# Decay attention followed by a token and channel mixer: w1 is loaded and converted one place later, and the token sums begin in pair 5

## The chip, the core and the metric

The kernel runs on one core of one Trainium2 chip. The metric is the device time of one execution in microseconds (us). The runs shown of the kernel before are 551.95, 554.14 and 551.8 us; their median is 551.95. Profiles come from one execution taken by the hardware profiler; its times are counted from the start of its span.

## The reference

Inputs are q, k and v of shape (4 batches, 8 heads, 768 positions, 64), one decay per head, and four weights. All are float32. The first half is attention with a decay and no softmax, in blocks of 64 positions:

```python
intra = einsum('bhic,bhjc->bhij', qb, kb) * Dmask          # lam ** (i - j) below the diagonal
out   = einsum('bhij,bhjd->bhid', intra, vb) + einsum('bhid,bhde->bhie', qb * lam_pow, kv_state)
kv_state = lam_block * kv_state + einsum('bhsd,bhse->bhde', kb * rev_pow, vb)
```

The heads are laid side by side into x of shape (4, 768, 512), and the second half is a mixer:

```python
h  = relu(x.T @ w_tok1) @ w_tok2         # over positions: w_tok1 (768, 256), w_tok2 (256, 768)
u  = x + h.T
h2 = relu(u @ w_ch1) @ w_ch2             # over channels: w_ch1 (512, 1536), w_ch2 (1536, 512)
out = u + h2
```

w_tok1 and w_tok2 are called w1 and w2 below. They come as 64-bit floats, and the kernel makes float32 of them itself.

## The kernel before

**Pairs and places.** Two heads of one batch are a *pair*; there are 16, four for each batch. The loop from line 671 runs i from -2 to 15; one turn of it is called *place i* here. Place i does the scores of pair i+1 (`scores`), the outputs of pair i (`from_states`, `outputs`), the running state of pair i+1 (`state`), the turning of k and q of pair i+2 (`turn_k`, `turn_q`, `turn_q_rows`), and the turning back of pair i's outputs (`turn_back`). The scores `sc`, the outputs `xT`, the states `kv`, the turned tiles `kt`, `qt` and `xp`, and the sums `ph` and `pu` are PSUM tiles. Pair i's output goes to `uT` of its batch (4 x 768 words in each partition).

**Precision.** Products of the mixer are made of three products each: a high part times a high part, low times high, high times low. So each operand exists as a high and a low tile. `turn_back` writes the turned outputs as `xhi` (ScalarE, line 391) and `xlo` (VectorE, line 392). They are in tiles for two pairs each, tags `xhi` and `xlo` with two buffers; the tiles of pairs 4 and 5 are the third of each tag and reuse those of pairs 0 and 1.

**Token sums.** A first-layer sum (`token_hidden`, line 479) is 18 matmuls of 128x256 for 128 hidden rows and half of the channels of one batch; it needs the turned outputs of two pairs and the whole of w1 in `w1h`, `w1l`. Its result is split by ScalarE (line 483, `hh`) and VectorE (line 484, `hl`). The second layer (`pu`, line 516) is added to `uT`. The table `take` says how many of these groups run in each place, `early` how many of them ahead of the first turning back.

**w1 and w2.** w1 comes in three parts of 512 KB (`load_w1`, line 430) to `uT` of batch 3, which nothing else uses yet. `convert_w1` makes float32 of a part: one step on ScalarE (line 410), four on VectorE (lines 411 to 420) in the space of `uT` of batch 1, and then the split into `w1h` (ScalarE, line 402) and `w1l` (GpSimd, line 403). w2 comes whole, 1.5 MB (`load_w2`, line 447), in place 3 to `uT` of batch 2, and goes through the same steps in three parts from place 5 on. The steps wait in the list `waiting`, and `later(n)` takes the next n of them between the other work.

**Order.** The order on each engine is that of the code; there is no scheduler for it. SP issues nearly all loads, one after the other: for each place v of pair i+3, then k and q of pair i+4. From pair 5 on q is loaded as four DMAs of 32 partitions and is turned by VectorE (line 227); before, TensorE turns it. A matmul that starts a PSUM tile waits until the bank's last reader is done:

```python
def bank(tag, nm, n):                    # line 82
    if tag == "sh" and spare:
        tag = spare.pop()
    return ps.tile([P, n], F32, tag=tag, bufs={"xT": 1, "sh": 3}[tag], name=nm)
```

`spare` gets the bank of the pair's first outputs once in each place, and the first turning of keys takes it.

**Operand tiles.** In place 10 `build` (line 633) begins to fill tiles for the channel mixer, among them `B11h0`, `B11l0`, `B21h0` and `B21l0` in the pool `up` (128 x 768 each). Nothing is in them before that.

Of the kernel before, what the change touches and what calls it, by code (L numbers as in the profile page):

```python
# [10 lines left out]
F32R = mybir.dt.float32r  # L11
# [11 lines left out]
def kernel(  # L23
# [25 lines left out]
    DM = H * D  # L49
    FT = w_tok1.shape[1]  # L50
    FC = w_ch1.shape[1]
    P = 128
    NC = S // P
# [318 lines left out]
    def turn_back(i, g):  # L372

        b, p = pairs[i]
        half = p // 2
        if p % 2 == 0 and g == 0:
            x_of[b, half] = [
                tokp.tile([P, NC, DM // 2], F32R, tag=t, bufs=2, name=f"{t}{b}{half}") for t in ("xhi", "xlo")
            ]
        xhi, xlo = x_of[b, half]  # L380
        xp = bank("sh", f"xp{i}{g}", 3 * P)
        for c in range(3):
            nc.tensor.transpose(  # L383
                out=xp[:, c * P : (c + 1) * P],
                in_=chunks_of(uT[b][:, p], g)[:, c],
                identity=ident,
            )
        hi = xhi[:, g::2, (p % 2) * P : (p % 2 + 1) * P]
        lo = xlo[:, g::2, (p % 2) * P : (p % 2 + 1) * P]
        src = xp.rearrange("p (c e) -> p c e", e=P)  # L390
        nc.scalar.copy(out=hi, in_=src)  # L391
        nc.vector.tensor_sub(out=lo, in0=src, in1=hi.bitcast(F32))  # L392
# [35 lines left out]
    def load_w1(i):  # L428
        cs = slice(2 * i, 2 * i + 2)
        nc.sync.dma_start(  # L430
            out=words(3).rearrange("p (c f) -> p c f", c=NC)[:, cs],
            in_=w_tok1.bitcast(U32).rearrange("(c s) f -> s c f", s=P)[:, cs],
        )
# [28 lines left out]
    def token_hidden(b, half, kk):  # L462

        if half == 0 and kk == 0:
            if b % 2:
                both = hidp.tile([P, 2, NK, DM], F32R, tag="h1", name=f"h{b}")
                hid[b] = both[:, 0], both[:, 1]
            else:
                hid[b] = [hidp.tile([P, NK, DM], F32R, tag=f"{t}0", name=f"{t}{b}") for t in ("hh", "hl")]
        hh, hl = hid[b]  # L470
        xh, xl = x_of[b, half]
        cs = slice(half * DM // 2, (half + 1) * DM // 2)

        ph = bank("sh", f"ph{b}{half}{kk}", DM // 2)
        fs = slice(kk * P, (kk + 1) * P)
        i = 0
        for c in range(NC):
            for w, x in ((w1h, xh), (w1l, xh), (w1h, xl)):
                nc.tensor.matmul(  # L479
                    out=ph, lhsT=w[:, c, fs], rhs=x[:, c], start=(i == 0), stop=(i == 3 * NC - 1)  # L480
                )
                i += 1
        nc.scalar.activation(hh[:, kk, cs], ph, AF.Relu)
        nc.vector.scalar_tensor_tensor(
            out=hl[:, kk, cs], in0=ph, scalar=0.0, in1=hh[:, kk, cs].bitcast(F32), op0=ALU.max, op1=ALU.subtract
        )
# [170 lines left out]
    groups = deque(hidden[0] + hidden[1][:NK] + outs[0] + hidden[1][NK:] + outs[1])  # L657
    for b in range(2, B):
        groups.extend(hidden[b] + outs[b])
    take = {4: 2, 5: 2, 6: 2, 7: 5, 8: 4, 9: 4, 10: 5, 11: 2, 12: 2, 13: 4, 14: 3, 15: 2}  # L660
    early = {4: 2, 5: 1, 6: 1}
    behind = []
    SCAN_FIRST = (5,)
    LATE = 7
# [9 lines left out]
    for i in range(-2, NI):  # L674
# [19 lines left out]
        if i + 2 < NI:  # L694
# [4 lines left out]
                turns += [(turn_q_rows, 0), (turn_q_rows, 1)]  # L699
            if i == -2:  # L700
                turns.sort(key=lambda x: x[1])
            if i >= NP and turns:
                behind.append(turns.pop())
            for f, g in turns:
                f(i + 2, g)
# [7 lines left out]
        for n in range(3):  # L713
# [11 lines left out]
            if n == 0 and i + 2 < NI:  # L725
                scale_k(i + 2)
                if i == LATE:
                    late_turns.popleft()(i + 2)
        if i == -1:
            load_w1(0)  # L730
        if 0 <= i + 3 < NI and i >= -1:
            load_v(i + 3)
        if i + 4 < NI:
            load_kq(i + 4)
        if i in (-1, 0):
            load_w1(i + 2)
        if i == 3:
            load_w2()
        if 0 <= i < 3:
            convert_w1(i)  # L740
        if i == 5:
            weights[0] = group_tiles(0, False)
            w3 = words(3)
# [648 lines left out]
```

## Time and profile before

| | |
|---|---|
| median of the runs | 551.95 us |
| the profiled execution's own time | 550.69 us |
| its span | 548.9 us |
| TensorE busy | 536.1 us (98%) |
| VectorE busy | 433.5 us (79%) |
| ScalarE, GpSimd busy | 255.3 us, 272.1 us |
| TensorE's clock | 1.00 of full speed in every stretch shown (the 2.4 GHz level) |

The chain of work that ended last is TensorE for 88% and VectorE for 5%. The first 165 us are the pairs with the token sums between them; the rest is the channel mixer. Rows of a timeline give start, length, engine, line, operation and tiles, and in brackets how long the engine had been idle before and what ended that. An engine "SPq" is SP's queue of DMA issues: the length is that of the issue, and the landing is told apart.

### The profile page before, as it was taken

How to read it: one execution, taken by the hardware profiler on the slowest of the kernel's cores; microseconds unless marked ns; L12 is line 12 of the kernel's file. 1: busy time of each engine (PE TensorE's matmuls, PEld its weight loads, DVE VectorE, ACT ScalarE, POOL GpSimd, SP SyncE). 2: the span in 40 equal slices, each digit the busy share in tenths (PEclk: the TensorE clock that was granted, in tenths of full speed). 3: DMA queues.
4: the chain of work that ended last, by engine and by line, in shares of the span. 5: the costliest groups of instructions: out<-in, count | busy, mean ns of one | idle time of the engine just before them, and what ended most of it. 6: DMA issues, size and time to landing. Idle time of an engine off the chain costs nothing.

```text
span 548.9 us, 11606 instructions
## 1 busy us (share of the span) xinstructions
PE 536.1 (98%) x4588; PEld 521.1 (95%) x4588; DVE 433.5 (79%) x658; ACT 255.3 (47%) x514; POOL 272.1 (50%) x242
## 2 busy tenths in 40 slices
PE   5999999999999999999999999999999999999997
PEld 4879998999989999999999999999999999999996
DVE  5697699588787988788778888788777778778894
ACT  3673553455453444443444344453455555455431
POOL 5574462745213564534444354354476656568450
PEclk9999999999999999999999999999999999999999
DMA  9999994998102614442716200014855132220276
GB/s 183 254 209 171 234 208 71 206 174 150 38 24 92 248 43 149 142 149 52 269 44 234 93 0 1 1 29 66 209 115 160 57 116 59 102 92 0 33 154 122
DMA packets 163142, 65.25 MB, mean 119 GB/s; under 512 B 151056, under 2 KB 153360, under 8 KB 163088
## 3 DMA queue, kind: packets, MB, share of 16 engines
q1 hardware_dynamic: 157856, 63.33, 47.5%
q10 hardware_dynamic: 5232, 1.18, 1.0%
q8 instruction: 36, 0.59, 0.5%
q14 instruction: 18, 0.15, 0.1%
HBM read 47.71 MB, written 16.78 MB: 117 GB/s over the span
## 4 chain that ended last, share of the span: by engine, by line
PE 88%; DVE 5%; DMA 2%; ACT 2%; POOL 1%; SPq 1%; issue 1%; ACTq 0%; DVEq 0%; POOLq 0%
PE po L1071 22%; PE pa L845 13%; PE pc L845 9%; PE pb L845 7%; PE pa L1045 7%; PE pc L1045 5%; PE ph L479 5%; PE sc L315 3%; PE xT L355 3%; PE pd L845 3%; PE pu L516 2%; PE pu L499 2%; DMA qn<-in_q_dram 1%; PE xT L338 1%; PE kv L267 1%; PE xp L383 1%
## 5 line engine op out<-in xcount | busy, mean ns | idle before, releaser
L1084 DVE TENSOR_TENSOR uT<-po,uT 128x768 f32<-128x768 f32 x57 | 54.2, 952 | 17.0 <-PE po L1071 16.7
L860 ACT ACTIVATE c<-c 128x384 f32<-128x384 f32 x42 | 22.1, 526 | 59.2 <-DVE c L905 33.4
L1051 DVE TENSOR_TENSOR uT<-pa,uT 128x768 f32<-128x768 f32 x36 | 34.3, 954 | 9.9 <-PE pa L1045 9.0
L862 POOL TENSOR_TENSOR h22l<-c,h22h 128x384 fp32r<-128x384 f32 x14 | 14.4, 1030 | 41.6 <-ACT h22h L861 41.6
L1051 DVE TENSOR_TENSOR uT<-pc,uT 128x768 f32<-128x768 f32 x27 | 25.8, 954 | 11.6 <-PE pc L1045 11.6
L286 POOL COPY st<-sv 128x320 f32<-128x320 f32 x16 | 13.6, 851 | 40.2 <-DVE sv L275 40.2
L298 DVE TENSOR_TENSOR a<-sc,mask 128x768 f32<-128x768 f32 x32 | 29.1, 947 | 4.3 <-PE sc L315 4.3
L403 POOL TENSOR_TENSOR c1l<-cs,c1h 128x512 fp32r<-128x512 f32 x15 | 19.3, 1296 | 23.1 <-ACT c1h L402 23.1
L1071 PE MATMUL po<-h12h,c 128*128 128x384 f32 x112 | 28.7, 337 | 0.0
L1071 PE MATMUL po<-h11h,c 128*128 128x384 f32 x112 | 28.6, 336 | 0.0
L1071 PE MATMUL po<-h21h,c 128*128 128x384 f32 x112 | 28.6, 336 | 0.0
L1071 PE MATMUL po<-h22h,c 128*128 128x384 f32 x112 | 28.6, 336 | 0.0
L479 PE MATMUL ph<-xhi,w1h 128*128 128x256 f32 x96 | 28.2, 293 | 0.1
L355 PE MATMUL xT<-a,vn 128*64 128x128 f32 x384 | 27.3, 277 | 0.0
L479 PE MATMUL ph<-xlo,w1h 128*128 128x256 f32 x96 | 27.1, 283 | 0.0
L479 PE MATMUL ph<-xhi,w1l 128*128 128x256 f32 x96 | 27.1, 282 | 0.0
L315 PE MATMUL sc<-qT,kT 64*64 64x128 f32 x768 | 25.2, 277 | 1.0 <-ACT xhi L391 0.8
L315 PEld LDWEIGHTS sc<-qT,kT 64*64 64x64 f32 x768 | 21.4, 136 | 4.2 <-issue 1.7
L254 POOL TENSOR_TENSOR qs<-qT,lamp 128x640 f32<-128x640 f32 x16 | 25.2, 1573 | 0.3 <-PE pu L516 0.2
L392 DVE TENSOR_TENSOR xlo<-xp,xhi 128x384 fp32r<-128x384 f32 x32 | 17.5, 551 | 7.4 <-ACT xhi L391 7.3
L355 PEld LDWEIGHTS xT<-a,vn 128*64 128x64 f32 x384 | 20.4, 137 | 3.0 <-issue 3.0
L403 POOL TENSOR_TENSOR c<-cs,c 128x512 fp32r<-128x512 f32 x10 | 12.9, 1295 | 19.7 <-ACT c L402 19.7
(399 smaller groups left out, 1942.9 us busy)
## 6 DMA issues: line engine op xcount, KB each, us to landing
raw<-in_moe_w_ch_dram SPq DMA_DIRECT2D x20, 512.0 KB, 3.7
vn<-in_v_dram SPq DMA_DIRECT2D x16, 384.0 KB, 5.1
kn<-in_k_dram SPq DMA_DIRECT2D x30, 192.0 KB, 5.6
out_dram<-y SPq DMA_DIRECT2D x104, 48.0 KB, 1.9
qn<-in_q_dram SPq DMA_DIRECT2D x44, 96.0 KB, 4.0
dc1h<-c1h SPq DMA_DIRECT2D x4, 768.0 KB, 5.3
dc1l<-c1l SPq DMA_DIRECT2D x4, 768.0 KB, 6.6
c1hr<-dc1h SPq DMA_DIRECT2D x4, 768.0 KB, 4.2
```

The lines of the kernel that those rows point to most:

```text
L254: nc.gpsimd.tensor_mul(out=qss[i], in0=qTs[i][:, P:].rearrange("p (c i) -> p c i", i=P), in1=lamp[:, p, None, :].broadcast_to([P, NC - 1, P]),
L298: nc.vector.tensor_mul(out=a, in0=pair.rearrange("p h (c i) -> p h c i", i=P), in1=mask[:, 2 * p : 2 * p + 2, None, :].broadcast_to([P, 2, ...
L315: nc.tensor.matmul(out=sc[h][half(j), c * P : (c + 1) * P], lhsT=kTs[i][half(h), js], rhs=qTs[i][half(h), cs], start=True, stop=True,)
L355: nc.tensor.matmul(out=xT[half((h + o) % 2), y * P : (y + 1) * P], lhsT=vns[i][:, h, c, :], rhs=weights_of[i, c // 3, h][:, c % 3, :], sta ...
L403: nc.gpsimd.tensor_sub(out=lo, in0=src, in1=hi.bitcast(F32))
L479: nc.tensor.matmul(out=ph, lhsT=w[:, c, fs], rhs=x[:, c], start=(i == 0), stop=(i == 3 * NC - 1))
L845: nc.tensor.matmul(out=to, lhsT=w[:, t], rhs=x[:, t], start=(start and i == 0), stop=(i == 5), skip_group_check=not start,)
L860: nc.scalar.activation(src, src, AF.Relu)
L1045: nc.tensor.matmul(out=pair[x][:, t], lhsT=w[:, t], rhs=h, start=(start and i == 0), stop=(i == 2), skip_group_check=not start,)
L1051: nc.vector.tensor_add(out=ub, in0=pair[x], in1=ub)
L1071: nc.tensor.matmul(out=to, lhsT=w[:, jj, t * P : (t + 1) * P], rhs=h, start=(i == 0), stop=(i == 3 * JG - 1))
L1084: nc.vector.tensor_add(out=ub, in0=po, in1=ub)
```

## The change

- w1: `load_w1` runs at the end of places -1, 0 and 1, each time behind the loads of v, k and q. Before, it ran in place -1 ahead of them and again behind them, and in place 0. `convert_w1` is called in places 1 to 3 and not 0 to 2.
- Sums: `take` has none in place 4 and three instead of two in places 5 and 6. The sums themselves and their order are the same; place 7 takes five as before. In place 4 both halves of the keys are turned ahead of the rest (`if i in take`).
- Tiles: the turned outputs of pairs 4 and 5 are not in `xhi`, `xlo` but in the four operand tiles named above, the even chunks of positions in one tile and the odd ones in another. `turn_back` and `token_hidden` index the tiles by chunk parity.

```diff
--- before.py
+++ after.py
@@ -374,9 +374,14 @@
         b, p = pairs[i]
         half = p // 2
         if p % 2 == 0 and g == 0:
-            x_of[b, half] = [
-                tokp.tile([P, NC, DM // 2], F32R, tag=t, bufs=2, name=f"{t}{b}{half}") for t in ("xhi", "xlo")
-            ]
+            if (b, half) == (1, 0):
+                x_of[b, half] = [
+                    [up.tile([P, NH, DM // 2], F32R, tag=f"{o}{x}0", name=f"x{o}{x}") for x in "hl"]
+                    for o in ("B11", "B21")
+                ]
+            else:
+                whole = [tokp.tile([P, NC, DM // 2], F32R, tag=t, bufs=2, name=f"{t}{b}{half}") for t in ("xhi", "xlo")]
+                x_of[b, half] = [[x[:, o::2] for o in range(2)] for x in whole]
         xhi, xlo = x_of[b, half]
         xp = bank("sh", f"xp{i}{g}", 3 * P)
         for c in range(3):
@@ -385,8 +390,8 @@
                 in_=chunks_of(uT[b][:, p], g)[:, c],
                 identity=ident,
             )
-        hi = xhi[:, g::2, (p % 2) * P : (p % 2 + 1) * P]
-        lo = xlo[:, g::2, (p % 2) * P : (p % 2 + 1) * P]
+        hi = xhi[g][:, :, (p % 2) * P : (p % 2 + 1) * P]
+        lo = xlo[g][:, :, (p % 2) * P : (p % 2 + 1) * P]
         src = xp.rearrange("p (c e) -> p c e", e=P)
         nc.scalar.copy(out=hi, in_=src)
         nc.vector.tensor_sub(out=lo, in0=src, in1=hi.bitcast(F32))
@@ -477,7 +482,7 @@
         for c in range(NC):
             for w, x in ((w1h, xh), (w1l, xh), (w1h, xl)):
                 nc.tensor.matmul(
-                    out=ph, lhsT=w[:, c, fs], rhs=x[:, c], start=(i == 0), stop=(i == 3 * NC - 1)
+                    out=ph, lhsT=w[:, c, fs], rhs=x[c % 2][:, c // 2], start=(i == 0), stop=(i == 3 * NC - 1)
                 )
                 i += 1
         nc.scalar.activation(hh[:, kk, cs], ph, AF.Relu)
@@ -657,8 +662,8 @@
     groups = deque(hidden[0] + hidden[1][:NK] + outs[0] + hidden[1][NK:] + outs[1])
     for b in range(2, B):
         groups.extend(hidden[b] + outs[b])
-    take = {4: 2, 5: 2, 6: 2, 7: 5, 8: 4, 9: 4, 10: 5, 11: 2, 12: 2, 13: 4, 14: 3, 15: 2}
-    early = {4: 2, 5: 1, 6: 1}
+    take = {5: 3, 6: 3, 7: 5, 8: 4, 9: 4, 10: 5, 11: 2, 12: 2, 13: 4, 14: 3, 15: 2}
+    early = {5: 1, 6: 1}
     behind = []
     SCAN_FIRST = (5,)
     LATE = 7
@@ -699,7 +704,7 @@
                 turns += [(turn_q_rows, 0), (turn_q_rows, 1)]
             if i == -2:
                 turns.sort(key=lambda x: x[1])
-            if i >= NP and turns:
+            if i in take and turns:
                 behind.append(turns.pop())
             for f, g in turns:
                 f(i + 2, g)
@@ -726,18 +731,16 @@
                 scale_k(i + 2)
                 if i == LATE:
                     late_turns.popleft()(i + 2)
-        if i == -1:
-            load_w1(0)
         if 0 <= i + 3 < NI and i >= -1:
             load_v(i + 3)
         if i + 4 < NI:
             load_kq(i + 4)
-        if i in (-1, 0):
-            load_w1(i + 2)
+        if -1 <= i < 2:
+            load_w1(i + 1)
         if i == 3:
             load_w2()
-        if 0 <= i < 3:
-            convert_w1(i)
+        if 1 <= i < 4:
+            convert_w1(i - 1)
         if i == 5:
             weights[0] = group_tiles(0, False)
             w3 = words(3)
```


On SP the three loads of w1 move. The names are those of the pair whose v, k or q is loaded (`vn3` is v of pair 3); `uT3` with `in_moe_w_tok1` is a part of w1. Before, from the end of place -1 to that of place 1:


```order
L430 DMA uT3_63<-in_moe_w_tok1_dram 128x2x512
L157 DMA vn2_243<-in_v_dram 128x12x64
L137 DMA kn3_245<-in_k_dram 128x6x64 x2
L140 DMA qn3_246<-in_q_dram 128x6x64 x2
L430 DMA uT3_63<-in_moe_w_tok1_dram 128x2x512
L157 DMA vn3_365<-in_v_dram 128x12x64
L137 DMA kn4_367<-in_k_dram 128x6x64 x2
L140 DMA qn4_368<-in_q_dram 128x6x64 x2
L430 DMA uT3_63<-in_moe_w_tok1_dram 128x2x512
L157 DMA vn4_494<-in_v_dram 128x12x64
L137 DMA kn5_496<-in_k_dram 128x6x64 x2
L115 DMA qn5_497<-in_q_dram 32x24x32 x4
```


The same stretch with the change, to the third part of w1:


```order
L157 DMA vn2_242<-in_v_dram 128x12x64
L137 DMA kn3_244<-in_k_dram 128x6x64 x2
L140 DMA qn3_245<-in_q_dram 128x6x64 x2
L435 DMA uT3_63<-in_moe_w_tok1_dram 128x2x512
L157 DMA vn3_364<-in_v_dram 128x12x64
L137 DMA kn4_366<-in_k_dram 128x6x64 x2
L140 DMA qn4_367<-in_q_dram 128x6x64 x2
L435 DMA uT3_63<-in_moe_w_tok1_dram 128x2x512
L157 DMA vn4_486<-in_v_dram 128x12x64
L137 DMA kn5_488<-in_k_dram 128x6x64 x2
L115 DMA qn5_489<-in_q_dram 32x24x32 x4
L435 DMA uT3_63<-in_moe_w_tok1_dram 128x2x512
```


Each part now stands behind the five DMAs (v, two of k, two of q; seven with pair 5's q) that it stood ahead of.

On VectorE, place 5 with the states of pair 6 (`sv6`) at its head. `uT3<-uT2` are the steps on w2, `xlo10` (or `xB21h`, `xB21l`) the low halves of pair 5's turned outputs `xp50` and `xp51`, and `hl0<-ph...` the low halves of the token sums. Before:


```order
L275 SCALAR_TENSOR_TENSOR sv6_974<-keep_88,kv6_963 128x320
L227 STREAM_TRANSPOSE qT7_984<-qn7_746 128x768
L484 SCALAR_TENSOR_TENSOR hl0_837<-ph010_994,hh0_836 128x256
L411 TENSOR_SCALAR uT3_63<-uT2_62 128x512
L414 SCALAR_TENSOR_TENSOR uT3_63<-uT2_62,uT3_63 128x512
L392 TENSOR_TENSOR xlo10_886<-xp50_1023,xhi10_885 128x3x128
L417 TENSOR_SCALAR uT3_63<-uT3_63 128x512
L420 SCALAR_TENSOR_TENSOR uT3_63<-uT3_63 128x512
L392 TENSOR_TENSOR xlo10_886<-xp51_1034,xhi10_885 128x3x128
L484 SCALAR_TENSOR_TENSOR hl0_837<-ph011_1040,hh0_836 128x256
```


With the change:


```order
L275 SCALAR_TENSOR_TENSOR sv6_932<-keep_88,kv6_921 128x320
L227 STREAM_TRANSPOSE qT7_942<-qn7_739 128x768
L489 SCALAR_TENSOR_TENSOR hl0_953<-ph000_954,hh0_952 128x256
L416 TENSOR_SCALAR uT3_63<-uT2_62 128x512
L397 TENSOR_TENSOR xB21h_840<-xp50_982,xB11h_838 128x3x128
L419 SCALAR_TENSOR_TENSOR uT3_63<-uT2_62,uT3_63 128x512
L422 TENSOR_SCALAR uT3_63<-uT3_63 128x512
L489 SCALAR_TENSOR_TENSOR hl0_953<-ph001_993,hh0_952 128x256
L425 SCALAR_TENSOR_TENSOR uT3_63<-uT3_63 128x512
L397 TENSOR_TENSOR xB21l_841<-xp51_1015,xB11l_839 128x3x128
L489 SCALAR_TENSOR_TENSOR hl0_953<-ph010_1023,hh0_952 128x256
```


The first step on w2 stands behind one token sum as before, but now behind the first sum of all (`ph000`) instead of the third (`ph010`), and three low halves of sums stand in this place and not two.

## Rows read from the trace of the kernel before

**Rows 1.** The page's first part: busy time of the span, share, instructions.

```profile
PE 536.1 (98%) x4588; PEld 521.1 (95%) x4588; DVE 433.5 (79%) x658; ACT 255.3 (47%) x514; POOL 272.1 (50%) x242
```

**Rows 2.** Stretches, places 1 to 7: length, busy us (instructions) by engine, clock, DMA.

```profile
20.42:26.98 6.56, 6.52 (x131) 5.73 (x131) 5.37 (x10) 4.43 (x11) 2.47 (x3) 1.00 1.14 251
26.98:33.93 6.95, 6.71 (x131) 5.73 (x130) 6.85 (x11) 5.08 (x12) 5.45 (x5) 1.00 1.19 250
33.93:41.00 7.07, 6.14 (x126) 5.11 (x125) 6.77 (x11) 5.39 (x12) 4.95 (x5) 1.00 0.95 170
41.00:50.93 9.93, 9.93 (x161) 9.42 (x161) 6.79 (x12) 3.88 (x9) 6.59 (x6) 1.00 0.97 173
50.93:61.32 10.39, 10.15 (x161) 9.43 (x160) 6.78 (x12) 5.37 (x13) 1.87 (x2) 1.00 0.94 247
61.32:71.72 10.40, 10.16 (x162) 9.44 (x161) 8.78 (x17) 6.30 (x14) 4.73 (x4) 1.00 0.93 177
71.72:82.96 11.24, 11.13 (x155) 10.23 (x155) 10.02 (x15) 5.80 (x12) 8.33 (x6) 1.00 1.04 221
```

**Rows 3.** Waits of TensorE in the span: us, times, longest.

```profile
PE sc L315 <- ACT xhi L391: 0.8, 1, 0.8
PE xp L383 <- ACT kT L222: 0.5, 2, 0.2
```

**Rows 4.** Timeline, TensorE, place 4: start, us, instruction [idle before].

```profile
45.16 0.55 PE L217 MATMUL kt<-ident,kn 128*128 128x128 f32 x3
45.47 0.36 PE L479 MATMUL ph<-xhi,w1h 128*128 128x256 f32 x1
47.71 0.49 PE L217 MATMUL kt<-ident,kn 128*128 128x128 f32 x3
50.18 0.82 PE L383 MATMUL xp<-ident,uT 128*128 128x128 f32 x6
```

**Rows 5.** Timeline, VectorE, end of place 3 and place 4.

```profile
39.87 0.98 DVE L227 STREAM_TRANSPOSE qT<-qn 128x768 f32<-128x768 f32 x1 [0.27 <-DMA qn<-in_q_dram]
40.77 0.39 DVE L411 TENSOR_SCALAR uT<-uT 128x512 uint32<-128x512 uint32 x1
46.38 0.98 DVE L227 STREAM_TRANSPOSE qT<-qn 128x768 f32<-128x768 f32 x1
48.32 0.42 DVE L484 SCALAR_TENSOR_TENSOR hl<-ph,hh 128x256 fp32r<-128x256 f32 x1 [0.96 <-ACT hh L483]
```

**Rows 6.** Timeline of SP's issues; then landings of 42.87's pair, of 51.43.

```profile
14.44 0.84 SPq L430 DMA_DIRECT2D uT<-in_moe_w_tok_dram  x1
21.84 0.55 SPq L430 DMA_DIRECT2D uT<-in_moe_w_tok_dram  x1
27.96 1.48 SPq L430 DMA_DIRECT2D uT<-in_moe_w_tok_dram  x1
42.87 1.65 SPq L115 DMA_DIRECT2D qn<-in_q_dram  x1
51.43 0.53 SPq L447 DMA_DIRECT2D uT<-in_moe_w_tok_dram  x1
52.67 3.29 SPq L137 DMA_DIRECT2D kn<-in_k_dram  x1
DMA to landing us min/median/max: 3.4/3.6/3.9
DMA to landing us min/median/max: 8.3/8.3/8.3
```

**Rows 7.** Timeline, VectorE and ScalarE at w2's landing, place 5.

```profile
59.75 0.43 DVE L411 TENSOR_SCALAR uT<-uT 128x512 uint32<-128x512 uint32 x1 [1.08 <-DMA uT<-in_moe_w_tok_dram]
59.75 0.69 ACT L410 ACTIVATE uT<-uT 128x512 f32<-128x512 f32 x1 [1.11 <-DMA uT<-in_moe_w_tok_dram]
60.34 0.46 ACT L391 CAST xhi<-xp 128x384 fp32r<-128x384 f32 x1
60.84 0.56 DVE L392 TENSOR_TENSOR xlo<-xp,xhi 128x384 fp32r<-128x384 f32 x1
```


## The prediction

> **What bounds the kernel now.** I read the page's first part, then the stretches place by place, then TensorE's waits, then the instructions of places 3 to 5 in order of time, then SP's issues and their landings. In the first the reader is to see that TensorE is busy for 98% of the span and VectorE for 79% [rows 1]: nothing but TensorE's stream sets the time, the number of its instructions does not change here, and so the time moves only by what TensorE waits. A "place" below is one turn of the loop over pairs, from the first score product of one pair to that of the next. The stretches give the length of each [rows 2]. Place 1 takes 6.56 us with TensorE busy for 6.52. Places 2 and 3 take 6.95 and 7.07 with 6.71 and 6.14 busy: here VectorE is nearly full (6.85 and 6.77), since it narrows a part of w1 in each. Place 4 takes 9.93 and is TensorE from end to end, because two token sums run in it; places 5 and 6 (two sums each) take 10.39 and 10.40 and lose 0.24 each. TensorE's waits beyond the first 10 us are small: 0.8 us at the end of place 3, and twice 0.24 for a copy of turned keys [rows 3].
>
> So places 4 to 6 are TensorE-bound, and what matters is how long the work that is taken out of place 4 leaves it, and whether what place 5 needs is there when it starts three microseconds sooner. For that I read the loads. SP issues them one behind the other without a gap from 14 to 52 us [rows 6]. The last quarter of pair 6's q is issued at 42.87 and the longer of the two last landings takes 3.9 us, the shorter 3.4: the load is there at about 46.3. w2 is issued at 51.43 and takes 8.3 us: 59.73 [rows 6]. At 59.75 both VectorE and ScalarE start on it, after waiting 1.08 and 1.11 us with nothing else to do [rows 7]. w2 is thus already late by a microsecond in the old order, where the place begins at 50.93.
>
> **The change, part by part.** *w1 one place later.* On SP no DMA is added: 3 issues of 512 KB move, and five others (v, two of k, two of q; seven with pair 5's q) go ahead of each. Up to pair 5's q SP then has one w1 issue less, which took 0.84, 0.55 and 1.48 us [rows 6]; all loads up to there move forward by about that. The third part is now issued behind pair 5's q, so from pair 6 on SP has done the same work as before. The two bounds for w2's issue: 1.7 us earlier, if the loads of 14 to 37 us run at the pace of their fastest neighbours, and 0.5 us later, if the third part's issue costs its 1.48 again and slows its followers. I take 0.8 us earlier, near the middle and close to what the first of the issues cost: w2 lands at 59.73 - 0.8 = 58.9 (58.0 to 60.3).
>
> *Conversions.* Four steps on VectorE, two on ScalarE and one on GpSimd per part move from places 1 to 3 to places 2 to 4 (they straddle the end of their place). Place 2 then starts like place 1: 6.56, a gain of 0.39. It ends at 26.98 + 6.56 = 33.54. Place 3 still carries conversions at both its ends; TensorE alone needs 6.14 there, and it took 7.07. Its last wait is for pair 5's turned q [rows 3, 5], whose load comes forward by the 0.8 us above. I take 6.5 (between 6.14 and 7.07): place 4 starts at 40.05 instead of 41.00.
>
> *Place 4 without token sums.* It loses 2 x 2.23 us of TensorE: 47.71 to 50.18 is the second half of the keys, 0.24, and one sum, and 45.47 to 47.71 the other sum [rows 4]. That leaves 9.93 - 4.46 = 5.47. It does not get that short. VectorE was busy for 6.79 in it, of which the two sums' low halves (2 x 0.42 [rows 5]) go: 5.95, and the third conversion now falls at its end. And the next place's scores need pair 6's q, which lands at 46.3 (46.0 if SP is a little ahead) and is then turned for 0.98 us; before, that transpose started at 46.38, right at the landing, and nobody waited since TensorE was in its sums [rows 5]. So place 5 starts at about 46.9, place 4 takes 6.85 (bounds 5.95, VectorE alone, and 7.3, the load at its old time), 3.1 us less than before.
>
> *Place 5 with three sums.* Its order on TensorE is: 4.16 us to the keys (41.00 to 45.16 [rows 2, 4]), keys 0.31, sum 2.24, keys 0.24, first turned outputs 0.38 (half of 50.18 to 50.93), 0.4 until the keys are copied out (0.24 was the wait before [rows 3], behind work that now comes later), sum 2.24, second turned outputs 0.38: the third sum could begin at 46.9 + 10.35 = 57.2. But on VectorE the first step on w2 now stands ahead of the low half of the first turned outputs, and ahead of every later one; on ScalarE the same with the high halves. PSUM has three shared banks for these (line 82), and one more that serves the first keys of a place. The first sum and the keys have given theirs back by then; the third sum takes the bank of the first turned outputs, and that comes free only when VectorE has passed the w2 step. After w2's landing this took 61.40 - 59.73 = 1.67 us in the old run [rows 7]. So the third sum starts at 58.9 + 1.67 = 60.6, 3.4 us late, and place 5 ends at 60.6 + 2.3 = 62.9 instead of 61.32. This is a new wait of about 3.4 us on TensorE; behind VectorE's waiting step stand the low halves of the turned outputs and of the second sum, behind ScalarE's the scaled keys of the next pair, all of them done before place 6 asks for them.
>
> *Place 6 with three sums.* 10.40 + 2.24 = 12.64; it ends at 75.55. Before, six sums were done at 71.72, when place 7 began. Place 7 and later do the same work in nearly the same order; in place 7 VectorE has one step less ahead of its masks, and I count back the 0.1 us that TensorE idles there (11.24 less 11.13 [rows 2]; bounds 0 and twice that).
>
> *The turned outputs in the operand tiles.* The tiles are four that exist already; reads and writes are the same in number and shape. Cost nothing: they are read in place 6, and built again only from place 11 on. If that cover were gone, the first operand would wait for one sum, 2.24 us.
>
> The sum by places: -0.39 (2), -0.57 (3), -3.08 (4), +5.6 (5), +2.24 (6), -0.1 (7): +3.7 us. On the profiled execution's 550.69 us (span 548.9) that is 554.4. The median of the runs shown, 551.95, lies 1.26 above it, so on its scale 555.6.
>
> The 8.3 us for w2 carry the term. They are 1.5 MB at 190 GB/s, issued behind a long row of small loads [rows 6]. The Trainium skill ("DMA: Bandwidth & Descriptors", section "Bandwidth", with its rule for kernel authors) has transfers of 1 MiB and more at three quarters of the peak and measures 1 MB at 341 GB/s. By that rate w2 would take about 4.7 us (an estimate from that page), the landing would be near 55, and the third sum would not be held. The trace of this kernel disagrees with 8.3 us, and I go by it; the other case is the first rival.
>
> **Rivals.** *w2 comes in time.* If w2 lands 3.4 us sooner than I say, at 55.5 or before, because the queue ahead of it is emptier, place 5 takes 12.6 and the sum is -0.39 - 0.57 - 3.08 + 2.24 + 2.24 = +0.4: 552.3. For it: after 52.67 SP stood for 3.29 us on one k load behind w2 [rows 6], so w2 shares its time with nothing that SP issued later, and a lighter queue would shorten it. Against it: SP issues back to back, and no issue ahead of w2 is removed.
>
> *Place 4 becomes free and the change gains.* If VectorE's relief in place 2 is carried on and pair 6's q comes a full 1.7 us sooner, places 3 and 4 run at TensorE's pace, 6.14 and 5.47 to 5.95, and w2 holds nothing: -0.39 - 0.93 - 4.2 + 4.48 = -1.0, and with the 0.24 that places 5 and 6 each lost given back, -1.5: 550.4. This decides if both loads come 1.7 us or more sooner. For it: TensorE's own work allows it. Against it: place 3 with the same load on VectorE took 7.07.
>
> *The wait spreads.* If the third part of w1 behind pair 5's q pushes the loads back instead (w2 at 60.3, pair 6's q at 47) and SP's later pieces, one of which moves behind pair 12's loads, hold a place too, then +5 in places 2 to 6 and up to 1 in places 8 to 10: 558.
>
> **How the numbers follow.** Forecast 0.55, its own range with w2's landing from 58.0 to 60.3: +2.7 to +5.0, so 554.6 to 557. w2 in time: 0.25. Gain: 0.10. Spread: 0.10. The range of 8 in 10 is 551.2 to 557.5: it holds the forecast and the first rival and leaves out most of the other two. About 0.5% (2.8 us) is what can be told from no change: above 554.7 lie four fifths of the forecast and the last rival, 0.54; under 549.2 only the far half of the gain, 0.05; within, the first rival and the rest, 0.41.
>
> **What would show it.** Place 4 close to 6.9 us and place 5 close to 16; a wait of TensorE of about 3 us, late in place 5, for VectorE's low half of turned outputs; VectorE and ScalarE idle for about 4 us each until w2's DMA; w2's issue between 49.7 and 52. The forecast is wrong if w2 lands before 56, or if the third sum of place 5 takes a bank that is freed ahead of the w2 step.

## The result, and the profile after

The changed kernel takes 559.3 us (median of 6 executions, 558.58 to 561.8) where the kernel before, run beside it, takes 552.09: a ratio of 1.013, with an interval from 1.0106 to 1.0154. That is 7.2 us more. The prediction said 555.6, slower, with a range to 557.5: the direction came, and so did the wait that it named, but not the size. The two profiled executions stand further apart, 559.91 against 550.69, since the one of before lies 1.4 us under its median and the one of after 0.6 us above; the working below goes by these two, 9.2 us.

TensorE's busy time went up by 3.1 us though it has the same instructions; VectorE and ScalarE stand as they were. This is the first part of the page after, beside [rows 1]:

```profile
PE 539.2 (97%) x4588; PEld 523.7 (94%) x4588; DVE 433.7 (78%) x658; ACT 255.3 (46%) x514; POOL 270.9 (49%) x242
```

The same stretches as in [rows 2], places 2 to 7 of the kernel after (length, then busy us and instructions by engine, granted clock, DMA share, GB/s):

```profile
26.79:33.35 6.56, 6.52 (x131) 5.73 (x130) 5.36 (x8) 4.44 (x11) 4.44 (x4) 1.00 1.13 250
33.35:39.86 6.51, 5.92 (x125) 5.12 (x125) 6.19 (x11) 5.01 (x12) 4.39 (x5) 1.00 0.89 175
39.86:48.25 8.39, 6.04 (x124) 5.14 (x125) 6.38 (x11) 4.92 (x11) 5.02 (x5) 1.00 1.05 204
48.25:66.01 17.76, 14.41 (x179) 13.37 (x179) 9.81 (x18) 6.10 (x13) 6.19 (x6) 0.85 0.97 216
66.01:79.30 13.29, 13.05 (x179) 12.33 (x179) 7.99 (x14) 6.36 (x14) 3.70 (x4) 0.94 0.87 171
79.30:91.37 12.07, 11.12 (x156) 10.22 (x155) 10.92 (x14) 5.39 (x11) 7.12 (x6) 1.00 0.49 111
```

The reader is to see two things: the lengths of places 4 to 7, and the clock, which is no longer 1.00 in places 5 and 6. Against the forecast, in us:

| place | before | forecast | after |
|---|---|---|---|
| 2 | 6.95 | 6.56 | 6.56 |
| 3 | 7.07 | 6.5 | 6.51 |
| 4 | 9.93 | 6.85 | 8.39 |
| 5 | 10.39 | 16.0 | 17.76 |
| 6 | 10.40 | 12.64 | 13.29 |
| 7 | 11.24 | 11.14 | 12.07 |
| 8, 10 | 11.53, 10.68 | the same | 11.92, 11.04 |

Place 9 and all from place 11 on are as before within 0.03. The waits of TensorE after, where [rows 3] had 0.8 us and small ones:

```profile
PE ph L484 <- DVE xB21h L397: 3.1, 1, 3.1
PE sc L315 <- DVE qT L227: 2.0, 1, 2.0
PE pu L521 <- DVE uT L526: 1.9, 3, 1.0
```

The first of them is the forecast one. Here it is on the three engines after (TensorE, then VectorE, then ScalarE):

```profile
58.27 0.49 PE L388 MATMUL xp<-ident,uT 128*128 128x128 f32 x3
61.87 0.58 PE L484 MATMUL ph<-xhi,w1h 128*128 128x256 f32 x1 [3.10 <-DVE xB21h L397]
...
66.01 2.27 PE L315 MATMUL sc<-qT,kT 64*64 64x128 f32 x48
...
60.18 0.43 DVE L416 TENSOR_SCALAR uT<-uT 128x512 uint32<-128x512 uint32 x1 [4.18 <-DMA uT<-in_moe_w_tok_dram]
61.25 0.56 DVE L397 TENSOR_TENSOR xB21h<-xp,xB11h 128x384 fp32r<-128x384 f32 x1 [0.65 <-ACT xB11h L396]
...
60.18 0.67 ACT L415 ACTIVATE uT<-uT 128x512 f32<-128x512 f32 x1 [4.22 <-DMA uT<-in_moe_w_tok_dram]
```

VectorE and ScalarE stand for 4.2 us until w2 is there at 60.18. ScalarE's high half of the turned outputs comes behind its step on w2 and VectorE's low half behind that, and the third sum starts at 61.87, 1.69 us after the landing (the forecast took 1.67 from [rows 7]). But the sum then takes 4.14 us, to 66.01, and not the 2.23 of those in [rows 4]; the first scores of place 6 take 2.27 and not 1.54. The granted clock says why. Stretches of 2 us of the kernel after, columns as above:

```profile
58.00:60.00 2.00, 0.76 (x7) 0.53 (x5) 0.00 (x0) 0.00 (x0) 0.00 (x0) 1.00 1.29 263
60.00:62.00 2.00, 0.13 (x1) 0.14 (x1) 1.17 (x3) 1.82 (x5) 0.00 (x0) 0.68 0.65 139
62.00:64.00 2.00, 2.00 (x10) 2.00 (x11) 2.00 (x5) 0.61 (x2) 0.00 (x0) 0.50 1.09 174
64.00:66.00 2.00, 2.00 (x10) 1.78 (x9) 0.14 (x1) 0.33 (x1) 1.59 (x2) 0.50 1.08 239
66.00:68.00 2.00, 2.00 (x48) 2.00 (x50) 0.79 (x2) 0.96 (x2) 1.21 (x1) 0.61 1.31 220
68.00:70.00 2.00, 2.00 (x60) 1.83 (x54) 1.46 (x2) 0.17 (x1) 0.00 (x0) 1.00 1.12 155
```

TensorE had been at 1.00 (2.4 GHz) until it stood still at 58.8. In the wait the clock fell to 0.50 (1.2 GHz), TensorE ran the whole third sum at that level, and came back in the scores of place 6. This also explains most of the 3.1 us of busy time that was added: 1.91 in the sum and 0.73 in the scores. The Trainium skill ("TensorE: Matmul & The Clock Gate", section "Part 1: The HAM clock gate") has these same two levels and lets activity decide between them; the trace agrees. A slow stretch is no accident of the profiled execution: the mean granted clock over the span was 0.994 to 0.997 in all six runs of the changed kernel, and 0.999 or 1.00 in 47 of 50 runs of the kernel before.

The loads after, SP's issues from pair 5's q to w2, against [rows 6]:

```profile
31.85 4.14 SPq L115 DMA_DIRECT2D qn<-in_q_dram  x4
36.03 0.53 SPq L435 DMA_DIRECT2D uT<-in_moe_w_tok_dram  x1
...
41.74 2.59 SPq L115 DMA_DIRECT2D qn<-in_q_dram  x4
...
51.51 0.53 SPq L452 DMA_DIRECT2D uT<-in_moe_w_tok_dram  x1
```

And w2's time from issue to landing:

```profile
DMA to landing us min/median/max: 8.6/8.6/8.6
```

Before, the last two issues of pair 5's q ended at 37.32:

```profile
34.73 2.59 SPq L115 DMA_DIRECT2D qn<-in_q_dram  x2
```

After, they end at 35.99, and then the third part of w1 stands in the way. Pair 6's q is out at 44.33, only 0.2 us before the old time (42.87 + 1.65 = 44.52), and w2 is issued at 51.51, where it was 51.43. So a head start of 1.3 us was used up before it reached w2.

One execution does not fix the sizes of such shifts. Seven of the executions below and above have the same program up to the end of place 4 (the changed kernel and experiments 2, 4, 8 and 9 to 11). In them place 3 took 6.50 to 7.95 us and place 4 took 7.78 to 9.10, VectorE began to turn pair 6's q at 46.96 to 48.91, and w2 (issue and landing time added) was there at 60.1 to 62.0.

### The profile page after: what moved, and what is told of

Read it like the earlier page. It is cut to its first block, busy times and chain, and to the rows that moved or that the text cites. A ratio compares the mean times of both kernels' runs of the same rounds, so it can differ in the third digit from the quotient of the medians.

```text
span 558.1 us, 11619 instructions
## 1 busy us (share of the span) xinstructions
PE 539.2 (97%) x4588; PEld 523.7 (94%) x4588; DVE 433.7 (78%) x658; ACT 255.3 (46%) x514; POOL 270.9 (49%) x242
## 4 chain that ended last, share of the span: by engine, by line
PE 85%; DVE 5%; DMA 4%; SPq 3%; issue 1%; ACT 1%; POOL 1%; ACTq 0%; DVEq 0%; POOLq 0%
PE po L1074 21%; PE pa L848 12%; PE pc L848 9%; PE pb L848 7%; PE pa L1048 7%; PE pc L1048 5%; PE ph L484 5%; PE pd L848 3%; PE sc L315 3%; DMA qn<-in_q_dram 3%; PE xT L355 3%; PE pu L521 2%; SPq L115 2%; DMA uT<-in_moe_w_tok_dram 2%; PE pu L504 1%; PE xT L338 1%
## 5 line engine op out<-in xcount | busy, mean ns | idle before, releaser
L484 PE MATMUL ph<-xhi,w1h 128*128 128x256 f32 x84 | 25.5, 304 | 3.3 <-DVE xB21h L397 3.1
L484 PE MATMUL ph<-xlo,w1h 128*128 128x256 f32 x84 | 24.5, 292 | 0.0
L484 PE MATMUL ph<-xhi,w1l 128*128 128x256 f32 x84 | 24.5, 292 | 0.0
L865 POOL TENSOR_TENSOR h21l<-c,h21h 128x384 fp32r<-128x384 f32 x14 | 17.4, 1246 | 9.1 <-POOL h22l L865 4.2
```

What stands on the lines that cost most here:

```text
L484: nc.tensor.matmul(out=ph, lhsT=w[:, c, fs], rhs=x[c % 2][:, c // 2], start=(i == 0), stop=(i == 3 * NC - 1))
L865: nc.gpsimd.tensor_sub(out=hl, in0=src, in1=hh.bitcast(F32))
```

## The experiments

Each time stands beside runs of the kernel before on the same chip, whose median was 551.3 to 552.0. Place lengths are from the profiled execution, whose loads differ by up to 2 us from one execution to the next. So a single mechanism is read from the place it acts in, and the ratio tells of the whole.

**1. w1 back at its old places, the sums and tiles as changed.**

```diff
+        if i == -1:
+            load_w1(0)
...
-        if -1 <= i < 2:
-            load_w1(i + 1)
+        if i in (-1, 0):
+            load_w1(i + 2)
...
-        if 1 <= i < 4:
-            convert_w1(i - 1)
+        if 0 <= i < 3:
+            convert_w1(i)
```

> The changed kernel with the loads and the conversions of w1 back at their old places; the sums begin in place 5 and the tiles are as changed. Theory (w2's landing holds the third sum of place 5, and the clock falls in that wait): places 2 and 3 take 6.95 and 7.07 us again, place 4 about 6.5, w2 lands at about 59.7, TensorE waits longer (about 3.9 us) for the same end, the third sum again takes 4.1 us: place 6 starts at about 65.5 and the time is 558.8. Rival (the third part of w1 behind pair 5's q is what makes pair 6's q and w2 late): place 5 ends 2 to 3 us sooner, 556.

Measured: 558.1 us, ratio 1.0105 (1.0086 to 1.0124). Places 2 to 6 take 6.95, 7.51, 6.69, 17.60 and 12.55. TensorE, third sum of place 5 and first scores of place 6:

```profile
62.11 0.58 PE L484 MATMUL ph<-xhi,w1h 128*128 128x256 f32 x1 [3.27 <-DVE xB21h L397]
65.95 1.54 PE L315 MATMUL sc<-qT,kT 64*64 64x128 f32 x48
```

The theory holds. Place 4 is shorter by 1.7 us, places 2 and 3 are longer by 1.4, and place 5 begins where it did (48.35 against 48.25). Its end is where it was too (65.95 against 66.01), because w2's landing sets it: VectorE starts on w2 at 60.42, 1.69 us ahead of the third sum, as in the changed kernel. The clock falls again, though not in the wait but right behind it. The wait and the third sum:

```profile
58.84:62.11 3.27, 0.00 (x1) 0.00 (x1) 1.04 (x3) 1.69 (x5) 0.00 (x0) 1.00 1.03 210
62.11:65.95 3.84, 3.84 (x18) 3.71 (x18) 2.28 (x5) 1.08 (x3) 1.29 (x2) 0.56 1.00 185
```

The wait of 3.27 is smaller than the 3.9 that I expected, since place 5 began at 48.35 and not at 47.5. The price, 6.2 us here and 7.2 in the changed kernel with intervals that overlap, is thus for the most part that of the sums' new places, not of w1's.

**2. The first step on w2 behind the third sum.**

```diff
-            waiting.extend(2 * idle + steps[0][:5] + idle + steps[0][5:] + steps[1][:2] + idle)
+            waiting.extend(10 * idle + steps[0] + steps[1][:2])
...
-            waiting.extend(steps[1][2:5] + idle + steps[2][:2] + idle + steps[1][5:] + steps[2][2:] + idle)
+            waiting.extend(steps[1][2:5] + steps[2][:2] + steps[1][5:] + steps[2][2:])
```

> The changed kernel with eight more empty turns ahead of the first step on w2, so that it stands behind the third sum of place 5, and without the four empty turns further on, so that the last step stands where it did. Theory: no wait for VectorE in place 5 (-3.1 us), the granted clock stays at 1.00 there, and so the third sum takes 2.23 instead of 4.14 and the first scores of place 6 1.54 instead of 2.27 (-2.6): 553.6. Rival 1 (the steps only hold something later): the wait comes back in place 6 or 7, 556.5 to 559. Rival 2 (the clock falls for another reason): the third sum still takes 4.1 us, 556.2.

Measured: 554.32 us, ratio 1.004 (1.0027 to 1.0054); place 5 takes 12.59. TensorE at the end of place 5, the third sum without a wait and the scores at full clock:

```profile
58.34 0.37 PE L484 MATMUL ph<-xhi,w1h 128*128 128x256 f32 x1
...
60.67 1.54 PE L315 MATMUL sc<-qT,kT 64*64 64x128 f32 x48
```

Moving w2's steps removes the wait and the slow clock together: 2.4 us remain over the kernel before, of 7.2. These 4.8 us are the largest part of the loss, and shown. The wait did not come back in place 6 or 7 (rival 1), and the clock did not fall for another reason (rival 2): its mean was 0.999 or 1.00 in all five runs. The two profiled executions stand 5.7 us apart (559.91 and 554.17), which is what was expected; the medians stand 5.0 apart. Places 7, 8 and 10 still take 11.92, 11.96 and 11.04, as in the changed kernel. The last step on w2 does not stand where it did, as the expectation has it: VectorE does it at 80.07, behind the first add of place 7 (79.60), and no longer ahead of it.

**3. w2 loaded a place earlier** (`load_w2` at i == 2 in place of 3).

> The changed kernel with w2 loaded one place earlier, behind pair 6's q and ahead of pair 6's v. Theory: w2 is issued near 44.4 and there by 54, no step waits for it, the wait of 3.1 and the slow clock (2.6) go: 553.6. Rival (the loads behind w2 are needed as much): pair 7's q lands 3 us or more later and VectorE stands for it in place 5: the third sum is late again by 1 to 3 us, 555 to 559.

Measured: 559.89 us, ratio 1.0141 (1.0117 to 1.0165). My theory for this run failed, and the rival was right in kind. Nobody waits for w2 any more, but pair 6's v, issued 0.6 us behind it at 46.92, takes 9.2 us, and TensorE needs it for the state in place 5:

```profile
56.25 1.33 PE L267 MATMUL kv<-vn,kd 128*64 128x64 f32 x20 [3.97 <-DMA vn<-in_v_dram]
```

Pair 7's q, the rival's load, is late as well: VectorE stands 1.52 us for it and turns it at 60.03 (53.38 in the changed kernel). The clock falls here too, behind another wait with another cause:

```profile
56.00:58.00 2.00, 1.75 (x27) 1.78 (x29) 0.31 (x1) 0.00 (x0) 0.00 (x0) 0.56 0.81 122
```

The load right behind w2 pays in either order: in the kernel before and the changed one that is pair 7's v, with 9.1 and 9.3 us, while pair 6's v takes 4.2 and 4.4. Loading w2 sooner moves that cost to another load, and here to one that TensorE needs.

**4. TensorE kept busy in the wait.** The second turning of pair 5's outputs is repeated seven times more; nothing else changes.

```diff
-        for c in range(3):
+        for c in [0, 1, 2] * (8 if (i, g) == (5, 1) else 1):
```

> The changed kernel with the second turning of pair 5's outputs repeated seven times more (21 matmuls, about 2.6 us), which fills TensorE's wait ahead of the third sum of place 5 and computes nothing new. Theory (the clock falls since TensorE stands still): the third sum starts at 61.9 as before but takes about 2.3 us instead of 4.14, the first scores of place 6 1.54 instead of 2.27: 556.7. Rival (the sum is slow for another reason, or the clock falls at that time whatever TensorE does): 559.3, or more by what the filling delays.

Measured: 558.45 us, ratio 1.0121 (1.0101 to 1.014): by time alone not told apart from the changed kernel. The places tell it. TensorE in the timeline, then the stretch of the third sum (columns as above):

```profile
59.60 2.78 PE L388 MATMUL xp<-ident,uT 128*128 128x128 f32 x24
62.95 0.39 PE L484 MATMUL ph<-xhi,w1h 128*128 128x256 f32 x1 [0.57 <-DVE xB21h L397]
...
65.30 1.54 PE L315 MATMUL sc<-qT,kT 64*64 64x128 f32 x48
```

```profile
62.95:65.30 2.35, 2.35 (x18) 2.21 (x19) 2.29 (x5) 0.96 (x3) 0.00 (x0) 1.00 0.90 142
```

w2 landed at 61.25 here, so the sum starts 1.70 us after the landing, as in the changed kernel (1.69). But it takes 2.35 us at a clock of 1.00, and the scores 1.54: 1.79 and 0.73 less, with the wait for w2 untouched. So the slow clock is a second price of standing still, and not of the sum or of the moment. The profiled execution gained 1.4 us over that of the changed kernel and not 2.5, because w2 landed 1.07 us later in it; why the median gained only 0.85 and not the 2.6 expected is not shown. The clocks of the runs agree: the mean was 1.00 in three of the four, and 0.995 in the slowest (560.11), against 0.994 to 0.997 in the six of the changed kernel.

**5. The loads of w1 alone, in the kernel before.** Loads one place later, sums and conversions in the old places.

```diff
-        first()
-        waiting.extend(steps)
+        waiting.extend([first] + steps)
...
-        if i == -1:
-            load_w1(0)
...
-        if i in (-1, 0):
-            load_w1(i + 2)
+        if -1 <= i < 2:
+            load_w1(i + 1)
```

> The kernel before, with only the three loads of w1 one place later on SP; conversions run in the old places, each part's first step on ScalarE one turn later so that it does not stand waiting; sums and tiles as before. Theory (the loads of pair 5's q come about 1.2 us sooner, as in the changed kernel, and the two sums of place 4 go on covering pair 6's q): place 3 takes 6.5 instead of 7.07, place 4 stays at 9.9, and the time is 551.3, under both kernels. Rival (a part of w1 lands behind its conversion, which then holds VectorE and the sums of place 4): place 4 takes 10.5 or more, 552.5 to 554.

Measured: 551.16 us against 551.47, ratio 0.9999 (0.9987 to 1.0012): no change. Neither theory holds. Place 4 stays at 9.93, but places 2 and 3 take 7.21 and 7.19. The order of the loads by itself gives nothing. The 0.39 that the change wins in place 2 is VectorE's conversions leaving, as the prediction had it: place 2 takes 6.56 or 6.57 in all nine executions that have them a place later, and 6.95 to 7.21 in the five that do not.

**6. The tiles alone, in the kernel before.**

> The kernel before, with only the turned outputs of pairs 4 and 5 moved into the operand tiles. Both theories, as the prediction had it: no instruction is added or moved, 552.0, within 0.2% of the kernel before. If reads of the new tiles cost anything, it is in places 4 to 6.

Measured: 551.51 against 551.47, ratio 1.0002 (0.9993 to 1.0011), places 4 to 6 at 9.93, 10.39 and 10.38. They cost nothing.

**7. The changed kernel without the third load of w1.**

```diff
-        first, *steps = narrow(raw[:, i * n : (i + 1) * n], tmp[:, :n], tmp[:, n:])
+        first, *steps = narrow(raw[:, min(i, 1) * n : (min(i, 1) + 1) * n], tmp[:, :n], tmp[:, n:])
...
-        if -1 <= i < 2:
+        if -1 <= i < 1:
             load_w1(i + 1)
```

> The changed kernel without the load of the third part of w1 (512 KB); the second part is converted twice in its place, so the sums are of other numbers. Theory (from 14 to 52 us the loads go at the pace of the DMA engines, and a part of w1 anywhere costs all that is issued behind it its bytes): pair 6's q and w2 come 1.2 to 2 us sooner, place 4 takes 6.9, w2 lands near 58.5, and the time is 557.5. Rival (only SP's issue of 0.53 us counts): 0.5 us sooner, 558.8.

Measured in one execution: 557.93 us. The stretch of place 4, and VectorE's turning of pair 6's q:

```profile
40.45:47.29 6.84, 5.86 (x125) 5.17 (x125) 6.38 (x11) 4.11 (x9) 3.81 (x4) 1.00 0.97 163
```

```profile
46.16 0.98 DVE L227 STREAM_TRANSPOSE qT<-qn 128x768 f32<-128x768 f32 x1 [0.35 <-DMA qn<-in_q_dram]
```

The same turning in the changed kernel:

```profile
47.13 0.98 DVE L227 STREAM_TRANSPOSE qT<-qn 128x768 f32<-128x768 f32 x1 [1.35 <-DMA qn<-in_q_dram]
```

Without the load, pair 6's q and w2 (59.23 against 60.18) come 1.0 us sooner, and place 4 takes the 6.84 that was forecast. Both come sooner, and place 4 is shorter, than in any of the seven executions that have the load behind pair 5's q (46.96, 60.1 and 7.78 at the least). Experiments 1 and 12, where the load stands ahead of pair 5's q, agree: place 4 takes 6.69 and 7.15. So the third part of w1 behind pair 5's q makes place 4 longer, by 0.6 to 2.4 us over these executions. It is not only the issue of 0.53 us (the rival): from issue to landing pair 5's v, the next load on SP, takes 5.6 to 6.4 us in the nine executions with this part of w1 right ahead of it, and 4.2 to 4.5 in the five without. The size for pair 6's q and w2 stays open, since 1.0 us between two single executions is less than executions of one program differ.

**8. Order of VectorE in place 7.**

```diff
-            waiting.extend(steps[1][2:5] + idle + steps[2][:2] + idle + steps[1][5:] + steps[2][2:] + idle)
+            waiting.extend(steps[1][2:5] + steps[2][:2] + steps[1][5:] + steps[2][2:] + idle)
```

> The changed kernel with one thing altered: of the empty turns between the steps on w2 that run in place 6 two go, one of them to the end, so that in place 7 one step on w2 and not two stands behind the running state on VectorE, as in the kernel before. The wait in place 5 and the slow clock stay. Theory (order alone costs TensorE 0.8, 0.4 and 0.4 us in places 7, 8 and 10): those places go back to 11.2, 11.5 and 10.7 and the time falls by 1.5, to 557.8. Rival (the steps come late because w2 does, so moving them only moves the wait): places 6 and 7 together stay at 25.4 and the time within 0.5 of the changed kernel's 559.3.

Measured: 556.8 us, ratio 1.0103 (1.0083 to 1.0123). Places 7, 8 and 10 take 11.13, 11.52 and 10.65. (Two empty turns go; the one at the end stood there before.) VectorE behind the state of place 7, in the changed kernel, and TensorE's second product group there:

```profile
83.85 0.80 DVE L275 TENSOR_TENSOR_SCAN sv<-keep,kv 128x320 f32<-128x320 f32 x1
84.58 0.40 DVE L422 TENSOR_SCALAR uT<-uT 128x512 f32<-128x512 f32 x1
85.01 1.15 DVE L425 SCALAR_TENSOR_TENSOR uT<-uT 128x512 uint32<-128x512 uint32 x1
86.07 0.55 DVE L526 TENSOR_TENSOR uT<-pu,uT 128x384 f32<-128x384 f32 x1
...
86.67 0.44 PE L521 MATMUL pu<-w2h,hh 128*128 128x384 f32 x1 [0.95 <-DVE uT L526]
```

And VectorE in this run:

```profile
80.59 0.80 DVE L275 TENSOR_TENSOR_SCAN sv<-keep,kv 128x320 f32<-128x320 f32 x1
81.31 0.66 DVE L425 SCALAR_TENSOR_TENSOR uT<-uT 128x512 uint32<-128x512 uint32 x1
82.53 0.56 DVE L526 TENSOR_TENSOR uT<-pu,uT 128x384 f32<-128x384 f32 x1 [0.56 <-PE pu L521]
```

With three sums in place 5 `later` is called at other points than with two, and one step more on w2 slid behind the state, ahead of the add that gives TensorE its bank. The theory holds for places 7, 8 and 10: 1.7 us by order alone. It does not rest on one pair of executions: place 7 takes 12.07 to 12.11 in the five that have the changed kernel's order there, and 11.23 or 11.24 in the three of experiments 5 and 6 and the kernel before. The 2.5 us between the medians are not all the order's. In this execution place 5 began 1.65 us later and took 14.27: the wait was 1.41 us and the clock stayed at 1.00 in place 5. It had fallen in place 4 (last section).

**9 to 11. Both repairs together.** Three kernels put w2's steps behind the sums of place 5 and take more of them by the end of place 6: the first with 8 empty turns and `later(1)`, the second with 10 and `later(2)`, the third like the second with one empty turn behind it.

```diff
+            waiting.extend(8 * idle + steps[0] + steps[1][:2])     # 10 in the second and third
... (the next line of `waiting` as in experiment 2)
+            later(1)                                              # later(2) in the second and third
+            waiting.extend(idle)                                  # third only
```

> The kernel with the steps on w2 behind place 5's sums, but with six more empty turns instead of eight and one more step taken at the end of place 6, so that in place 7 VectorE has one step less ahead of the second-layer adds, as in the kernel before. Theory (the order of VectorE in places 7 to 10 costs 0.8, 0.4 and 0.4 us there): places 7, 8 and 10 go back to 11.2, 11.5 and 10.7, and the time is 552.8. Rival (the steps are late because w2 is late, whatever their order): 554.3 again, with the waits of TensorE for VectorE's adds still 1.1 us or more.

> The kernel whose first step on w2 stands behind the third sum of place 5, with two more steps taken at the end of place 6, so that VectorE's order from place 7 on is that of the kernel before. Theory: both losses go that come from the order of VectorE; place 5 takes 12.6, place 6 12.9, places 7, 8 and 10 take 11.2 to 11.6, 11.5 and 10.7: 553.0, the rest over the kernel before being place 4, which stands for pair 6's q. Rival (as in the kernel with six empty turns, the steps are only squeezed into place 6 and 7, which then take 13.7 and 13.1): 555.5 to 556.5.

> The kernel with the steps on w2 behind place 5's sums and two more steps at the end of place 6, with one empty turn behind them, so that the first step on the next weights stands behind two of VectorE's adds in place 7, where the kernel before has it. Theory (the order of VectorE in place 7 alone made the 13.2 there): place 7 takes 11.2, places 5 and 6 stay at 12.6 each, 553.0 to 554.0; what is left over the kernel before is place 4. Rival (VectorE has too much in places 6 and 7 in any order): place 7 stays above 12, 555 to 556.

Measured: 556.16, 556.06 and 554.26 us, ratios with intervals from 1.007 to 1.0099, 1.0072 to 1.0107 and 1.004 to 1.0066; place 7 takes 13.07, 13.24 and 11.87, places 8 and 10 are back at 11.5 and 10.65 in all three. In the first the time is above both theory and rival (place 6 takes 13.67). In the second the rival's time came, though place 6 takes 12.57 and not 13.7. In both I took one step too many, and now a step on the next weights stands between VectorE's second and third adds of place 7, which ran one behind the other before. VectorE and TensorE in the second:

```profile
84.04 0.52 DVE L526 TENSOR_TENSOR uT<-pu,uT 128x384 f32<-128x384 f32 x1
84.48 1.64 DVE L416 TENSOR_SCALAR uT<-uT 128x512 uint32<-128x512 uint32 x1
...
86.64 0.44 PE L521 MATMUL pu<-w2h,hh 128*128 128x384 f32 x1 [1.18 <-DVE uT L526]
```

In the third the order is that of experiment 8, and more than half of it comes back; 11.87 and not 11.2, so a part of the rival stands: the steps that were put off end later, and VectorE begins the masks of place 7 3.52 us into it (2.88 in the kernel before). It is no faster than experiment 2.

**12. The third of these, with w1 at its old places as well.**

> The same kernel with the loads and conversions of w1 at their old places too; three sums in places 5 and 6 and none in place 4 remain. Theory (the third part of w1 ahead of pair 6's q makes place 4 long by 1.5 us, its absence brings back 1.0 in places 2 and 3): place 4 takes 6.7, the others as told, 552.5, still a little over the kernel before by TensorE's idle in place 4. Rival (the change's idea, not its details, costs nothing): 551.3 or less, no slower than the kernel before.

Measured: 553.49 against 551.27 us, ratio 1.0039 (1.0026 to 1.0053). Places 4 to 6 (columns as above):

```profile
41.44:48.59 7.15, 5.85 (x124) 5.15 (x125) 6.43 (x11) 3.92 (x9) 4.07 (x4) 1.00 0.93 159
48.59:61.19 12.60, 12.35 (x179) 11.64 (x179) 6.37 (x10) 4.57 (x11) 5.36 (x5) 1.00 1.02 240
61.19:73.89 12.70, 12.46 (x180) 11.62 (x179) 9.03 (x16) 6.93 (x15) 3.33 (x3) 1.00 0.92 185
```

With no late w2 and no slow clock the three still take 32.45 us and not 30.72 [rows 2]: TensorE is idle for 1.30 of the 7.15 in place 4 (5.85 busy), since pair 6's q sets its end, while places 5 and 6 got the two sums in full. VectorE turns that q, and TensorE's next scores start at 48.59, behind it:

```profile
47.47 0.98 DVE L227 STREAM_TRANSPOSE qT<-qn 128x768 f32<-128x768 f32 x1 [0.67 <-DMA qn<-in_q_dram]
```

The rival is out: taking the sums out of place 4 costs 1.7 us in places 4 to 6 by itself. Place 7 adds 0.6 (11.85), so not all of this run's loss is the idea's. No kernel here beat the one before; the nearest, experiments 5 and 6, equal it.

## Why the prediction went wrong in size

*Right.* Place 2 to within 0.01 (experiment 5). The order of place 5: the third sum takes the bank of the first turned outputs, stands behind the step on w2, and starts 1.69 us after the landing (1.67 said; 1.68 to 1.70 in the five executions that have this wait). The tiles cost nothing (experiment 6). Both sums of place 4 reappear in full in places 5 and 6, and nothing fills place 4. The rivals "w2 comes in time" and "place 4 becomes free" did not come.

*Right by luck.* Place 3 took 6.51 where 6.5 was said, but 6.50 to 7.95 in seven executions of the same program up to there; and [rows 3] put its last wait down to ScalarE's `xhi` and not to pair 5's q. TensorE's wait of 3.10 us came out close to the 3.4 since two misses cancel in it: place 5 began 1.35 us later than said (48.25 for 46.9), and w2 came 1.28 later (60.18 for 58.9).

*Given too little.* Both conditions of "the wait spreads" came, w2 at 60.18 (60.3 said) and pair 6's q turned from 47.13 (47 said), and places 8 to 10 lost 0.76 us together (up to 1 said). It had a chance of 0.10, and its 558 is the nearest of the four times to the 559.3 measured. The loss in places 8 to 10 has another cause than it gave: order on VectorE (experiment 8), not SP's pieces. A reading beside the first rival does not hold either, that w2 shares its time with nothing that SP issued later: pair 7's v was issued at 52.06, 0.6 us behind w2, and took 9.1 us, so both were under way together. No number rests on it.

*Wrong, in order of size*, on the scale of the profiled executions, 9.2 against 3.7 us:

- The step "place 5 ends at 60.6 + 2.3": the sum was priced at full clock although TensorE stands for three microseconds ahead of it. It took 4.14 and the next scores 2.27: 2.5 us over the terms of the sum (2.3 for the third sum, 12.64 for place 6), and in no rival either. Experiment 4 shows that it is the standing still: with TensorE busy and w2 as late, the same sum took 2.35.
- The step "place 7 and later do the same work in nearly the same order", counted as -0.1: the order did differ, by one step on VectorE, and TensorE waits for it: 0.9 over the forecast in place 7 and 0.4 each in places 8 and 10. Experiment 8 shows 1.7 us for one changed line.
- The step "I take 0.8 us earlier" for w2: it landed at 60.18, not 58.9, 1.3 us on the end of place 5. It was issued 0.9 later than said (51.51 for 50.6) and took 8.6 us for 8.3. The third part of w1, now behind pair 5's q, takes back what the first part's move gave; without it both w2 and pair 6's q came 1.0 us sooner (experiment 7, one execution). For the same reason place 4 took 8.39 and not 6.85; that cost nothing further, since TensorE waits 3.10 us for w2 behind it.

These are 2.5 + 1.7 + 1.3 = 5.5 us, which is what was missing.

The loss as a whole, then: the wait with its slow clock 4.8 us of 7.2 (experiment 2). The rest is order in places 7 to 10, and TensorE idle in place 4; their shares overlap in the repairs, and no run undoes both of them at once without adding something of its own: how the last 2.4 us divide stays open.

## What to carry to other kernels

A wait of the engine that sets the time can have a second price: look at the granted clock right behind it, and cost the work that follows at the lower level. Before work is moved out of a stretch, ask what load that stretch was covering; here the two sums hid pair 6's q, and w2's late landing was hidden by work that came ahead of it. And where steps are fed in turn by turn, a change in the number of turns shifts everything behind it: compare the order on each engine beyond the stretch that was meant to change.

## What was not expected of the hardware

The clock fell from 1.00 to 0.50 in TensorE's wait of 3.10 us in the changed kernel, and within 1 us behind the end of waits of 3.11, 3.27 and 3.97 (experiments 7, 1 and 3). It stayed at 1.00 in and behind waits of 0.57, 1.41, 1.98 and 2.02 (experiment 4, place 5 of experiment 8, and the ends of place 4 in the changed kernel and in experiment 4). But the length of the wait alone does not decide. In experiment 8 it also fell behind a wait of 2.00 us, ahead of place 4, where TensorE was busy for 7.46 us and not 6.04. The scores behind the wait, and all of place 4:

```profile
41.71 1.94 PE L315 MATMUL sc<-qT,kT 64*64 64x128 f32 x48 [2.00 <-DVE qT L227]
```

```profile
41.71:49.90 8.19, 7.46 (x124) 6.57 (x125) 6.38 (x11) 3.93 (x9) 4.61 (x4) 0.79 1.04 191
```

How much of the following work is slow differed too: the scores of place 6 took 2.27, 1.67 and 1.54 us in the changed kernel and experiments 7 and 1.

VectorE's step L416 on 128x512 words took 0.43 us in place 5 of the changed kernel, where GpSimd did nothing, and 1.64 in place 7 of the second kernel of experiments 9 to 11, where GpSimd was at work; whether that is the cause was not tried.
